# Attention with cached K and V: K loaded as four heads in 4 KB rows, V as one head per transfer

## The chip, the cores and the metric

The kernel runs on one core of a Trainium2 chip. A core has a matrix engine (TensorE, "PE" in the profile, with its weight loads as "PEld"), VectorE (DVE), ScalarE (ACT), GpSimd (POOL), a queue that mainly starts transfers (SyncE, SP) and 16 DMA engines that move data between the main memory and the core's SBUF. The metric is the time of one execution in device microseconds; a lower time is better.

## The reference

Two independent blocks, A and B, each compute an attention layer with a given cache:

```python
q = (x @ wq).reshape(B, Sq, H, Dh).transpose(0, 2, 1, 3)
scores = einsum("bhqd,bhkd->bhqk", q, k_cache) * (Dh ** -0.5)
p = softmax(scores, axis=-1)
o = einsum("bhqk,bhkd->bhqd", p, v_cache)
out = o.transpose(0, 2, 1, 3).reshape(B, Sq, H * Dh) @ wo
```

with B = 16 batches, Sq = 64 queries, D = 640, H = 32 heads, Sk = 512 keys and Dh = 128, all in bf16. The result is A's and B's output side by side, 16 x 64 x 1280. K and V of both blocks are 268 MB, each byte read once.

## The kernel before

**Steps.** A step works on one head of two batches, whose 2 x 64 queries fill 128 partitions. There are 512 steps: two blocks, two halves of 16 heads, eight pairs of batches, 16 heads. Two steps make a macro-step m (256 in all), and two macro-steps make a group of four heads, k (128 in all).

**One macro-step** goes through these operations, which the code names by short codes:

- LDK loads K (512 KB): two heads of two batches, on the partitions head by head with 64 partitions each, in rows of 8 keys, which are 2 KB. `kn_ring` has nine such buffers.
- KX (L586) transposes K on TensorE in 32 pieces of 64 rows of 128 elements, and KE (L593) copies the result from PSUM to `ktp_ring`, which has three slots (slot 0 for even m, slots 1 and 2 in turn for odd m).
- SM (L632) multiplies queries and transposed K, one matmul for each batch of a step, on two halves of the partitions; MX (L641) takes the negative row maximum on VectorE; EX (L647) takes the exponential on ScalarE and sums the rows; RC2 (L653) takes the reciprocals.
- NM (L661) on GpSimd multiplies the probabilities by the reciprocals and puts them into the order of the keys that V has on the partitions.
- TR2 (L670) transposes the probabilities on TensorE; TE and TA (L680, L684) copy them to SBUF.
- LDV loads V, one transfer of 512 KB for four heads of one batch, so two for each k: partition p holds keys 4p to 4p + 3 of each head, which is a row of 1 KB for each head. `v_ring` has five buffers for groups.
- PV2 (L694) multiplies V and the transposed probabilities; OE4 (L701) copies the result of four heads from PSUM.
- OP2 and OX (L709, L719) multiply by `wo`, and add up over 16 heads in PSUM; OVP, OXP, OVF, OXF and ST write out halves and sums.
- Q projections (QJ, QZ, QN, L603) and the transposes of x (XI, XT) stand in between.

**Order.** The order on each engine is written out by hand. `PHASES` holds, for a range of k, a template for each of TensorE, ScalarE, VectorE and GpSimd: operation, offset in macro-steps, sub-index and a time within a period. `build_plan` turns it into one list for each engine. All four SM groups of a k stand together at the start of its period.

**Transfers.** All loads are issued from the SP queue, in an order that `build_plan` works out from planned times (`STEP_US`, `DMA_US`, `START_US`): a load is due `LEAD` macro-steps before the operation that first needs it, not before its buffer is free. Each load is also tied to the TensorE operation that stands at its planned time ("paced"), so that SP waits for TensorE's progress. Waits are semaphores: each load adds 16 to the semaphore of its buffer when it has landed, and TensorE, which works in order, waits for it ahead of the operation that reads the buffer.

The two lines that matter for the shape of the V and K transfers are these:

```python
src = blocks[blk][2][2 * bp + m % 2, h0:h0 + G].rearrange("g (p t) d -> p g (t d)", p=128)
src = blocks[blk][1][2 * bp:2 * bp + 2, h0:h0 + 2].rearrange("j hs (p t) d -> (hs p) j (t d)", t=8)
```

Of the kernel before, what the change touches and what calls it, by code (L numbers as in the profile page):

```python
# [15 lines left out]
class Cfg:  # L16
    G = 4
# [5 lines left out]
    LEAD = 5.37  # L23
    WLEAD = 5.48
    STEP_US = ((8, 3.68), (32, 27.17), (160, 3.12), (216, 3.1), (256, 3.43))
    DMA_US = dict(LDK=1.40, LDV=1.44, LDWQ=1.8, LDWO=1.8, LDX=0.45, LDXR=0.5)
    START_US = 210.96
    BEFORE = 3.88
# [17 lines left out]
         (("OE4", -4, 0, 0.38), ("QEZ", 0, 0, 0.43), ("QEZ", 0, 1, 1.68), ("OVP", -1, 0, 2.62), ("QEZ", 0, 2, 2.72),  # L46
          ("EX", 1, 0, 2.78), ("QEZ", 0, 3, 3.12), ("QEZ", 0, 4, 3.5), ("EX", 1, 1, 3.54), ("QEZ", 0, 5, 3.88),
          ("EX", 0, 1, 4.51), ("OXP", -13, 0, 4.63), ("QEJ", 4, 0, 4.64), ("TA2", -2, 0, 4.76), ("EX", 0, 0, 5.06),
          ("QEZ", 0, 7, 5.11), ("QEN", -6, 0, 5.12), ("QEZ", 0, 6, 5.49), ("ST", -45, 0, 6.19)),
         (("KE", 4, 0, 0.07), ("XIE", 2, 1, 0.91), ("MX", 0, 0, 0.95), ("MX", 0, 1, 0.96), ("RC2", -1, 0, 0.99),  # L50
          ("MX", 1, 0, 1.46), ("OXF", 47, 0, 2.01), ("MX", 1, 1, 2.78), ("OVF", -23, 0, 3.45), ("TE2", -1, 0, 3.61),
          ("XIE", 2, 2, 3.73), ("XIE", 2, 3, 3.96), ("KE", 3, 0, 4.55), ("XIE", 6, 0, 4.58), ("XIE", 0, 4, 4.84),
          ("XIE", -4, 6, 4.98), ("XIE", -2, 5, 5.43), ("RC2", 0, 0, 5.63), ("XIE", 0, 7, 6.21)),
# [6 lines left out]
         (("OE4", -4, 0, 0.38), ("QEZ", 0, 0, 1.23), ("OXP", -13, 0, 1.5), ("EX", 0, 1, 1.52), ("OVP", -17, 0, 1.59),  # L60
          ("EX", 0, 0, 1.89), ("XTE", 28, 0, 2.28), ("QEZ", 0, 1, 2.45), ("QEN", -6, 0, 2.53), ("ST", -35, 0, 3.16),
# [22 lines left out]
          ("QEN", -6, 0, 3.07), ("TA2", -2, 0, 3.72), ("OXP", -3, 0, 4.37), ("OVP", -3, 0, 4.78), ("EX", 1, 1, 5.06),  # L84
          ("XTE", 0, 0, 5.27)),
         (("KE", 3, 0, 0.07), ("RC2", -1, 0, 0.53), ("MX", 0, 0, 1.15), ("MX", 0, 1, 1.7), ("MX", 1, 0, 1.78),
          ("KE", 2, 0, 2.61), ("MX", 1, 1, 3.18), ("RC2", 0, 0, 3.78), ("OXF", -3, 0, 4.23), ("TE2", -1, 0, 4.74),
          ("OVF", -3, 0, 5.58)),
# [9 lines left out]
          ("OXF", -3, 0, 6.18)),  # L98
# [12 lines left out]
    )  # L111
    TRB = (2, 3)
    OXB = 4
    OXH = False
    KTB = (6, 6)
    NWU = 32

# [22 lines left out]
def build_plan(dims, cfg):  # L140
# [73 lines left out]
    def bank(i):  # L214
        return ("PB", i)
# [173 lines left out]
    def sem_key(op):  # L389
        if op.kind in ("LDK", "LDV", "LDXR"):  # L390
            return ("d_" + op.kind[2:].lower(), op.writes[0][1])
# [542 lines left out]
```

## Time and profile before

| | |
|---|---|
| median of 3 runs | 850.43 us (849.04 to 854.05) |
| the profiled execution | 852.97 us |
| its span | 851.0 us |
| instructions | 38,366 |
| read from main memory | 292.03 MB |
| K: transfers, size, issue to landing (median, block A) | 128 per block, 512 KB, 6.5 us |
| V: transfers, size, issue to landing (median, block A) | 128 per block, 512 KB, 6.8 us |
| issue of one V transfer on SP (median) | 0.368 us |
| scores, L632 | 1,024 matmuls, mean 385 ns |
| normalizing, L661 | 512 on GpSimd, mean 843 ns |

The span is the time from the first to the last instruction of the one profiled execution; the execution's own time is 2 us longer. The table of the page counts busy time by engine; two engines can be busy at once, so shares don't add up to 100%. A packet is one contiguous row that one of the 16 DMA engines moves. The profile gives for each queue of the DMA engines the packets, the megabytes and the time its packets took, as a share of the span of all 16 engines; it can exceed 100% because packets of one engine may overlap a little.

### The profile page before, as it was taken

The page shows a single profiled execution, that of the slowest core. Times are in us where ns is not written, and L with a number is a line of the kernel's source. Part 1 is how long each engine was busy: PE and PEld are TensorE (multiplying, and loading weights), DVE is VectorE, ACT ScalarE, POOL GpSimd, SP SyncE. Part 2 cuts the span into 40 slices and gives each one's busy share as a digit, 9 for nine tenths or more (in the row PEclk, how much of TensorE's full clock was granted, in tenths as well). Part 3 has the DMA queues.
Part 4 walks back from the last instruction along what each step waited for, and adds up shares of the span by engine and source line. Part 5 has one row for each costly group of instructions (what it writes and reads, how often), then busy time and mean ns, then how long its engine had stood idle before and what let it go on. Part 6 is the DMA issues. An engine that isn't in the chain of part 4 may idle for free.

```text
span 851.0 us, 38366 instructions
## 1 busy us (share of the span) xinstructions
PE 811.3 (95%) x17025; PEld 566.4 (67%) x17156; DVE 727.9 (86%) x1192; ACT 644.7 (76%) x1466; POOL 417.1 (49%) x518
## 2 busy tenths in 40 slices
PE   8999999999999999999999998999999999999996
PEld 5566676666666666666666666666666666666664
DVE  4688888888888898888899887988888989989994
ACT  2678877777777787777877877787887877778886
POOL 0355455454544554454554545455455455455553
PEclk9999999999999999999999999999999999999999
DMA  9999999999999999999999999999999999999992
GB/s 306 360 354 349 369 354 352 348 338 362 354 352 353 369 369 363 359 360 367 364 362 367 364 360 349 321 362 362 360 360 363 366 369 365 366 339 352 370 321 89
DMA packets 228438, 297.14 MB, mean 349 GB/s; under 512 B 9136, under 2 KB 162736, under 8 KB 228272
## 3 DMA queue, kind: packets, MB, share of 16 engines
q1 hardware_dynamic: 225968, 292.06, 100.3%
q8 instruction: 134, 2.20, 1.1%
q10 hardware_dynamic: 2304, 2.62, 0.9%
q14 instruction: 32, 0.26, 0.1%
HBM read 292.03 MB, written 2.62 MB: 346 GB/s over the span
## 4 chain that ended last, share of the span: by engine, by line
PE 89%; issue 3%; ACT 3%; DMA 2%; DVE 2%; SPq 0%; ACTq 0%
PE ps L586 17%; PE ps L694 15%; PE ps L603 15%; PE ps L632 14%; PE ps L670 13%; PE ps L709 12%; PE ps L719 3%; ACT p_ring L647 2%; DMA v_ring<-in_A_v_cache_dram 1%; DVE negmax L641 1%; ACT pT_ring L684 1%; DMA wq_sb<-in_A_wq_dram 1%; DVE ktp_ring L593 1%; PE ps L804 0%; PE ps L813 0%
## 5 line engine op out<-in xcount | busy, mean ns | idle before, releaser
L661 POOL TENSOR_SCALAR pn_ring<-p_ring,recip 128x512 bf16<-128x512 bf16 x512 | 416.4, 843 | 425.1 <-DVE recip L653 379.0
L647 ACT ACTIVATE p_ring<-ps,negmax 128x512 bf16<-128x512 f32 x512 | 349.0, 688 | 74.0 <-DVE negmax L641 68.5
L593 DVE COPY ktp_ring<-ps 128x2048 bf16<-128x2048 bf16 x256 | 312.1, 1219 | 56.3 <-PE ps L586 56.2
L641 DVE TENSOR_REDUCE negmax<-ps 128x1 f32<-128x512 f32 x512 | 328.3, 683 | 16.2 <-PE ps L632 8.5
L586 PEld LDWEIGHTS ps<-ident,kn_ring 64*128 64x128 bf16 x8192 | 136.8, 95 | 107.9 <-issue 96.4
L586 PE MATMUL ps<-ident,kn_ring 64*128 64x64 bf16 x8192 | 169.2, 191 | 3.3 <-issue 1.4
L603 PE MATMUL ps<-xT_sb,wq_sb 128*128 128x512 bf16 (+2 forms) x543 | 133.4, 372 | 19.0 <-issue 18.1
L670 PEld LDWEIGHTS ps<-ident,pn_ring 128*128 128x128 bf16 x2048 | 125.4, 98 | 38.8 <-ACT p_ring L647 7.2
L694 PE MATMUL ps<-pT_ring,v_ring 128*128 128x64 bf16 x4096 | 143.5, 194 | 2.8 <-issue 1.9
L701 ACT ACTIVATE oT_ring<-ps 128x512 bf16<-128x512 f32 x128 | 76.4, 597 | 91.7 <-PE ps L694 91.7
L684 ACT ACTIVATE pT_ring<-ps 128x1024 bf16<-128x1024 bf16 (+1 forms) x144 | 140.9, 987 | 3.0 <-DVE pT_ring L680 2.2
L670 PE MATMUL ps<-ident,pn_ring 128*128 128x128 bf16 x2048 | 138.9, 219 | 3.4 <-issue 1.6
L709 PE MATMUL ps<-wo_sb,oT_ring 128*128 128x512 bf16 x498 | 135.3, 379 | 4.0 <-issue 1.9
L632 PE MATMUL ps<-ktp_ring,qc_ring 128*64 128x512 bf16 x1024 | 135.5, 385 | 0.7 <-issue 0.7
L694 PEld LDWEIGHTS ps<-pT_ring,v_ring 128*128 128x128 bf16 x4096 | 128.2, 98 | 9.6 <-issue 2.4
L647 ACT ACTIVATION_READ_ACCUMULATOR p_ring<-ps,negmax 128x1 f32 x512 | 104.8, 205 | 0.0
L680 DVE COPY pT_ring<-ps 128x1024 bf16<-128x1024 bf16 (+1 forms) x128 | 82.5, 644 | 14.6 <-PE ps L670 14.1
L619 ACT ACTIVATE qc_ring<-ps 128x512 bf16<-128x512 f32 (+1 forms) x129 | 76.8, 596 | 21.5 <-PE ps L603 21.4
L603 PEld LDWEIGHTS ps<-xT_sb,wq_sb 128*128 128x128 bf16 x660 | 53.8, 98 | 54.0 <-issue 1.1
L632 PEld LDWEIGHTS ps<-ktp_ring,qc_ring 128*64 128x64 bf16 x1024 | 47.2, 109 | 34.1 <-issue 1.3
L709 PEld LDWEIGHTS ps<-wo_sb,oT_ring 128*128 128x128 bf16 x512 | 42.7, 98 | 25.0 <-ACT pT_ring L684 2.1
L653 DVE RECIPROCAL recip<-rowsum 128x2 f32<-128x2 f32 x256 | 39.8, 155 | 4.4 <-ACT p_ring L647 4.4
(21 smaller groups left out, 127.2 us busy)
## 6 DMA issues: line engine op xcount, KB each, us to landing
kn_ring<-in_A_k_cache_dram SPq DMA_DIRECT2D x128, 512.0 KB, 6.5
v_ring<-in_A_v_cache_dram SPq DMA_DIRECT2D x128, 512.0 KB, 6.8
kn_ring<-in_B_k_cache_dram SPq DMA_DIRECT2D x128, 512.0 KB, 6.3
v_ring<-in_B_v_cache_dram SPq DMA_DIRECT2D x128, 512.0 KB, 6.5
wq_sb<-in_A_wq_dram SPq DMA_DIRECT2D x8, 640.0 KB, 7.1
wo_sb<-in_A_wo_dram SPq DMA_DIRECT2D x8, 640.0 KB, 7.2
wq_sb<-in_B_wq_dram SPq DMA_DIRECT2D x8, 640.0 KB, 6.8
wo_sb<-in_B_wo_dram SPq DMA_DIRECT2D x8, 640.0 KB, 6.6
```

The costliest lines, as they stand in the source:

```text
L586: last = e.transpose(kt_ps[hs][:, 64 * t:64 * t + 64], kn_ring[r, m % NKB, t // 8, t % 8 * DH:(t % 8 + 1) * DH], ident[r, r])
L593: ins = e.tensor_copy(ktp_ring[:, ktslot(op.idx)], ps[:, b:b + 2, :].rearrange("p b s -> p (b s)").bitcast(BF16))
L603: last = e.matmul(dst[:, col:col + n], wq_sb[:, qslot(hh // G), kt, (hh % G) * DH:(hh % G + 1) * DH], xT_sb[:, kt, lo * 128:hi * 128], sta ...
L632: ins = e.matmul(s_bank(g)[64 * j:64 * j + 64, :], q[:, 64 * j:64 * j + 64], kt[:, sub, j], start=True, stop=True, tile_position=(0, 64 * j))
L641: ins = e.reduce_max(negmax[:, r:r + 1], s_bank(g), axis=AX.X, negate=True)
L647: ins = e.activation(p_ring[:, g % NP, :], s_bank(g), ACTF.Exp, bias=negmax[:, r:r + 1], scale=1.0, accum_out=rowsum[:, r:r + 1])
L661: ins = e.tensor_scalar(dst, src, recip[:, r:r + 1], 1.0, ALU.mult, ALU.mult)
L670: ins = e.transpose(pt_flat(m)[:, (4 * sub + t) * 128:(4 * sub + t + 1) * 128], pn_ring[:, g % NPN, t * 128:(t + 1) * 128], ident[:, :])
L680: ins = e.tensor_copy(*pt_copy(op.idx, op.aux))
L684: ins = e.activation(*pt_copy(op.idx, op.aux), ACTF.Copy)
L694: ins = e.matmul(qo_ps[:, col:col + 64], v_ring[:, m // 2 % NVP, j, 2 * (m % 2) + sub, t * DH:(t + 1) * DH], pT_ring[:, m % NT, sub, t, 64 ...
L709: ins = e.matmul(out_ps, oT_ring[:, m // 2 % NO, 2 * (m % 2) + sub, :], wo_sb[:, wslot(ps_, hh // G), hh % G, 0:N0], start=(hh == 0), stop ...
```

## The change

Three things are changed together, with the order tables written anew.

- **K.** A K transfer now holds four heads of one batch, 32 partitions for each head, in rows of 16 keys, which are 4 KB. A macro-step's K buffer is thus no longer that of the macro-step's own two heads and two batches: the four heads of a k need both buffers of the pair, one for each batch. SM reads its head from two slots of `ktp_ring`, in 16 runs of 32 elements, and depends on both.
- **V.** A V transfer now holds one head of one batch (128 KB), so there are four times as many. Partition 32 th + p holds keys 16 p + 4 th to 16 p + 4 th + 3, which matches the order in which K's keys come out. PV2 waits for its own two heads of both batches only; a semaphore counts the four transfers of one PV2.
- **NM** writes the probabilities in four blocks of 32 for each run, instead of every second element.

The constants that plan the loads and the order tables are others; the sequence of operations within a period is nearly the same (for example OP2, OP2, OX where OP2, OX, OP2 stood).

```diff
-    LEAD = 5.37
-    WLEAD = 5.48
-    STEP_US = ((8, 3.68), (32, 27.17), (160, 3.12), (216, 3.1), (256, 3.43))
-    DMA_US = dict(LDK=1.40, LDV=1.44, LDWQ=1.8, LDWO=1.8, LDX=0.45, LDXR=0.5)
-    START_US = 210.96
-    BEFORE = 3.88
+    LEAD = 5.65
+    WLEAD = 5.95
+    STEP_US = ((8, 5.16), (32, 27.91), (160, 3.04), (216, 3.1), (256, 4.77))
+    DMA_US = dict(LDK=1.34, LDV=0.36, LDWQ=1.8, LDWO=1.8, LDX=0.45, LDXR=0.5)
+    START_US = 268.53
+    BEFORE = 4.65
...
         if kind == "SM":
-            return mk("pe", "SM", (m, sub), [qres(2 * m + sub), ("ktp", ktslot(m))], [bank(2 + (2 * m + sub) % cfg.NS)],
-                      ts)
+            return mk("pe", "SM", (m, sub), [qres(2 * m + sub), ("ktp", ktslot(2 * k)), ("ktp", ktslot(2 * k + 1))],
+                      [bank(2 + (2 * m + sub) % cfg.NS)], ts)
...
         if kind == "PV2":
-            return mk("pe", "PV2", m, [("pT", m % cfg.NT, 0), ("pT", m % cfg.NT, 1), ("v", k % cfg.NVP, 0), ("v", k % cfg.NVP, 1)], [bank(1)], ts)
+            return mk("pe", "PV2", m, [("pT", m % cfg.NT, i) for i in range(2)] + [("v", k % cfg.NVP, j, i) for j in range(2) for i in (g0 % G, g1 % G)], [bank(1)], ts)
...
-        add([("PV2", 2 * (k - cfg.NVP) + 1, 0)] if k >= cfg.NVP else [], ("PV2", 2 * k, 0), cfg.LEAD - j, 2, "LDV", m,
-            [("v", k % cfg.NVP, j)], m)
+        for i in range(G):
+            add([("PV2", 2 * (k - cfg.NVP) + i // 2, 0)] if k >= cfg.NVP else [], ("PV2", 2 * k + i // 2, 0), cfg.LEAD - j + i // 2, 2, "LDV", m,
+                [("v", k % cfg.NVP, j, i)], (m, i))
...
-        if op.kind in ("LDK", "LDV", "LDXR"):
+        if op.kind == "LDV":
+            return ("d_v", op.writes[0][1], op.aux[1] // 2)
+        if op.kind in ("LDK", "LDXR"):
...
-        kn_ring = sb("kn_ring", [128, NKB, 2, 8 * DH], BF16)
+        kn_ring = sb("kn_ring", [128, NKB, 16 * DH], BF16)
...
-            kt = ktp_ring[:, ktslot(m)].rearrange("p (hs j s) -> p hs j s", hs=2, j=2)
+            hd = 2 * (m % 2) + sub
...
+                kt = ktp_ring[:, ktslot(m // 2 * 2 + j)].rearrange("p (hs t h s) -> p hs t h s", hs=2, t=16, h=2)
                 ins = e.matmul(s_bank(g)[64 * j:64 * j + 64, :], q[:, 64 * j:64 * j + 64],
-                               kt[:, sub, j], start=True, stop=True, tile_position=(0, 64 * j))
+                               kt[:, hd // 2, :, hd % 2, :], start=True, stop=True, tile_position=(0, 64 * j))
...
-            src = p_ring[:, g % NP, :].rearrange("q (th tl pp) -> q th tl pp", th=2, tl=4)
-            dst = pn_ring[:, g % NPN, :].rearrange("q (tl pp th) -> q th tl pp", tl=4, th=2)
+            src = p_ring[:, g % NP, :].rearrange("q (th tl p) -> q th tl p", th=4, tl=4)
+            dst = pn_ring[:, g % NPN, :].rearrange("q (tl th p) -> q th tl p", tl=4, th=4)
...
-        def em_LDKV(e, op):
+        def em_LDK(e, op):
             m = op.aux
             blk, bp, grp, ps_, hh0 = step_info(2 * m)
             h0 = (ps_ % NHALF) * HH + hh0
-            if op.kind == "LDV":
-                h0 -= h0 % G
-                src = blocks[blk][2][2 * bp + m % 2, h0:h0 + G].rearrange("g (p t) d -> p g (t d)", p=128)
-                ins = e.dma_start(v_ring[:, m // 2 % NVP, m % 2], src)
-            else:
-                src = blocks[blk][1][2 * bp:2 * bp + 2, h0:h0 + 2].rearrange("j hs (p t) d -> (hs p) j (t d)", t=8)
-                ins = e.dma_start(kn_ring[:, m % NKB], src)
+            h0 -= h0 % G
+            src = blocks[blk][1][2 * bp + m % 2, h0:h0 + G].rearrange("h (p t) d -> (h p) (t d)", t=16)
+            ins = e.dma_start(kn_ring[:, m % NKB], src)
+            return ins, ins
+
+
+        def em_LDV(e, op):
+            m, i = op.aux
+            blk, bp, grp, ps_, hh0 = step_info(2 * m)
+            h = (ps_ % NHALF) * HH + hh0 - hh0 % G + i
+            src = blocks[blk][2][2 * bp + m % 2, h].rearrange("(p th t) d -> th p (t d)", th=4, t=4)
+            ins = e.dma_start(v_ring[:, m // 2 % NVP, m % 2, i], src)
             return ins, ins
```

More of the change, by code (lines that the diff above doesn't have):

```diff
@@ L39 @@
         (0,
[6 rows of a table removed]
[L46 to L53, printed above, removed]
[6 rows of a table removed]
-         (("OE4", -4, 0, 0.38), ("QEZ", 0, 0, 1.23), ("OXP", -13, 0, 1.5), ("EX", 0, 1, 1.52), ("OVP", -17, 0, 1.59),
-          ("EX", 0, 0, 1.89), ("XTE", 28, 0, 2.28), ("QEZ", 0, 1, 2.45), ("QEN", -6, 0, 2.53), ("ST", -35, 0, 3.16),
[22 rows of a table removed]
[L84 to L88, printed above, removed]
[9 rows of a table removed]
-          ("OXF", -3, 0, 6.18)),
[12 rows of a table removed]
[6 rows of a table added]
@@ new lines @@
+         (("OE4", -4, 0, 0.18), ("QEJ", 4, 0, 0.57), ("QEZ", 0, 0, 0.99), ("QEZ", 0, 1, 1.01), ("OVP", -9, 0, 2.27),
+          ("OXP", -7, 0, 2.33), ("EX", 1, 0, 2.75), ("QEZ", 0, 2, 3.35), ("QEZ", 0, 3, 3.38), ("ST", -53, 0, 3.41),
+          ("QEN", -6, 0, 3.77), ("EX", 1, 1, 3.84), ("QEZ", 0, 4, 4.01), ("EX", 0, 0, 4.55), ("QEZ", 0, 5, 4.62),
[3 rows of a table added]
+          ("XIE", 2, 2, 4.0), ("XIE", 2, 3, 4.35), ("XIE", 0, 4, 4.88), ("XIE", -4, 6, 5.23), ("XIE", 0, 7, 5.26),
[9 rows of a table added]
+          ("QEZ", 0, 2, 3.95), ("QEN", -6, 0, 4.46), ("EX", 1, 0, 4.8), ("OXP", -17, 0, 4.94), ("QEZ", 0, 3, 5.01),
+          ("EX", 1, 1, 5.79)),
+         (("MX", 0, 0, 0.18), ("OVF", -55, 0, 0.84), ("KE", 3, 0, 1.07), ("MX", 0, 1, 1.09), ("RC2", -1, 0, 1.12),
+          ("MX", 1, 0, 2.53), ("KE", 2, 0, 4.46), ("MX", 1, 1, 4.62), ("TE2", -1, 0, 4.76), ("RC2", 0, 0, 4.98),
+          ("OXF", 13, 0, 5.18)),
[7 rows of a table added]
+          ("OXP", -3, 0, 6.17), ("OVP", -3, 0, 6.24)),
[10 rows of a table added]
+          ("TA2", -2, 0, 3.63), ("QEN", -6, 0, 3.77), ("OVP", -3, 0, 4.49), ("EX", 1, 1, 5.23), ("OXP", -3, 0, 5.9),
+          ("XTE", 0, 0, 6.28)),
+         (("KE", 3, 0, 0.68), ("MX", 0, 0, 0.9), ("RC2", -1, 0, 0.91), ("MX", 0, 1, 1.47), ("MX", 1, 0, 2.66),
+          ("KE", 2, 0, 2.72), ("MX", 1, 1, 2.95), ("RC2", 0, 0, 4.13), ("TE2", -1, 0, 4.82), ("OVF", -3, 0, 5.04),
+          ("OXF", -3, 0, 5.65)),
[9 rows of a table added]
+          ("OXF", -3, 0, 5.93)),
[9 rows of a table added]
+          ("OXF", -77, 0, 5.93)),
+         (("NM", -1, 1, 3.23), ("NM", -1, 0, 4.58), ("NM", 0, 0, 5.12), ("NM", 0, 1, 6.06))),
@@ L585, in em_KX @@
                     r = slice(64 * hs, 64 * hs + 64)
-                    last = e.transpose(kt_ps[hs][:, 64 * t:64 * t + 64], kn_ring[r, m % NKB, t // 8, t % 8 * DH:(t % 8 + 1) * DH],
+                    last = e.transpose(kt_ps[hs][:, 64 * t:64 * t + 64], kn_ring[r, m % NKB, t * DH:(t + 1) * DH],
                                        ident[r, r])
@@ L839, in mha_kernel @@
                         OVP=em_OVP, OXP=em_OXP, OVF=em_OVF, OXF=em_OXF, ST=em_ST, INIT1=em_INIT1, INIT2=em_INIT2,
-                        LDWQ=em_LDWQ, LDWO=em_LDWO, LDX=em_LDX, LDXR=em_LDXR, XT=em_XT, XTE=em_XTE, XI=em_XI, XIE=em_XIE, WU=em_WU, LDK=em_LDKV, LDV=em_LDKV)
+                        LDWQ=em_LDWQ, LDWO=em_LDWO, LDX=em_LDX, LDXR=em_LDXR, XT=em_XT, XTE=em_XTE, XI=em_XI, XIE=em_XIE, WU=em_WU, LDK=em_LDK, LDV=em_LDV)
         def full(s, v):
```

98 rows, old and new, of the table PHASES are left out of this document.

## The prediction

> **What bounds the kernel now.** I read the page's first three parts, then the waits and the chain, then the DMA traffic of a stretch in the middle, and last the trace's record of single packets.
>
> ```profile
> PE 811.3 (95%) x17025; PEld 566.4 (67%) x17156; DVE 727.9 (86%) x1192; ACT 644.7 (76%) x1466; POOL 417.1 (49%) x518
> DMA  9999999999999999999999999999999999999992
> DMA packets 228438, 297.14 MB, mean 349 GB/s; under 512 B 9136, under 2 KB 162736, under 8 KB 228272
> q1 hardware_dynamic: 225968, 292.06, 100.3%
> PE 89%; issue 3%; ACT 3%; DMA 2%; DVE 2%; SPq 0%; ACTq 0%
> ```
>
> The reader is to see two resources that are full at once. TensorE is busy for 811.3 of 851.0 us and makes 89% of the chain. The 16 DMA engines carry packets for 100.3% of the span. TensorE hardly waits for them: the longest waits of this kind in the list of waits are 1.2 us (wq_sb, at the start) and 0.9 us (v_ring), once each, and of the longer waits of the SP queue nearly all are for TensorE, since the loads are paced by it. So the loads just keep up. A middle stretch shows how closely:
>
> ```profile
> 400.00:500.00 100.00, 97.16 (x2059) 67.61 (x2072) 89.23 (x146) 76.48 (x175) 50.45 (x62) 1.00 1.06 364
> ```
>
> Here PE (first figure after the length) is 97% busy at full clock, and DMA moves 364 GB/s with packet times that add up to 1.06 of its engines' time.
>
> The trace records each packet. Medians: 46 ns for 1 KB (44 at least), 55 for 1,280 B, 84 for 2 KB, 307 for 8 KB (the shortest), 1,085 for the 16 KB of instruction code, 9 for the 4 bytes that end an engine's share of a load. They are the same with three packets in flight as with twenty, so I read them as what one engine spends on one packet. Check on 400 to 500 us, which holds 19,026 packets of 1 to 1.25 KB, 7,778 of 2 KB, 1,137 ends and 16 of code: 19,026 x 46.7 + 7,778 x 84 + 1,137 x 9 + 16 x 1,085 = 1,570 us, over 16 engines 98 us of the 100. The medians explain a full queue.
>
> The 9,136 packets under 512 B are those ends. The kernel issues 571 transfers (256 K, 256 V, 32 weight tiles, 11 of x, 16 stores), and 571 x 16 = 9,136: every transfer of before runs on all 16 engines. In each of them both sides have 128 as their outermost dimension.
>
> **The change, part by part.**
>
> *V loads (LDV).* A transfer of 512 KB becomes four of 128 KB: 256 become 1,024, still of 1 KB rows, 131,072 packets. What is new is the shape of the source: the rows are taken as th (4) x p (32) x 1 KB, and in the built program the DRAM side reads 4 x 32 x 512 elements against 128 x 512 in SBUF. All other transfers keep 128 outermost on both sides. A transfer must be cut so that an engine's part of the source matches its part of the destination; along the outermost dimensions, 4 and 128, there are only four such parts. Every row of before fits a cut along the outermost dimension; none shows one that goes into an inner dimension, as sixteen parts of 4 x 32 would need. The built program also drops, on these 1,024 transfers alone, a mark that every other one carries. I therefore take the cut into four as the likely one: V then runs on 4 of the 16 engines.
>
> [...]
>
> The four engines' work, each of them:
> - V: 131,072 / 4 x 46 ns = 1,507 us (before: 131,072 / 16 x 46 = 377).
> - K, cut over 16 as before, now 32,768 packets of 4 KB. No row has 4 KB; between 84 (2 KB) and 307 (8 KB) a straight line gives 158, and bounds are 2 x 84 = 168 and 307 / 2 = 153. I take 159: 2,048 x 159 = 326 us (before 4,096 x 84 = 344), with 313 to 344.
> - wq 640 x 46 = 29; wo, x and stores 768 x 55 = 42; ends (1,024 + 315) x 9 = 12; code 134 / 16 x 1,085 = 9.
>
> Sum 1,925 us, against some 807 for each engine before.
>
> [...]
>
> *Path and covers.* Around that sum: about 2 us before the first packet and 2 us in which the early loads, which wait for TensorE, leave engines idle (DMA share 0.90 in the first 20 us); at the end about 2 us until the last load's semaphore, and what follows the last L694 group, at 844.7 of 851.0, so 6.3 us. Span 1,925 + 12 = 1,937. The profiled execution took 852.97 for its span of 851.0, and the median of the runs is 850.43: +2.0 - 2.5. I say 1,940.
>
> The four engines don't run dry: V's loads are paced about five macro-steps ahead of use, and while TensorE stands at a PV2 the loads of some two more batches of four heads (8 x 32 x 46 + 2 x 8 x 159 = 14.3 us of queue each) are already issued. One ring on SP feeds both kinds, so K's share on these engines lies behind V's and K comes late too. V late means PV2 (L694 before) waits on TensorE's in-order queue; behind it stand the next scores, K transposes and Q projections, for which VectorE, ScalarE and GpSimd wait. All of them idle together.
>
> *Scores (SM)* read K^T in 16 runs of 32 elements instead of one run of 512, and need both slots of a pair of K blocks. All four SM groups of a pair already run back to back after both K copies, so the second adds no wait. No row has such a read: bounds are no change and a doubling of 135.5 us. I take none, as nearest to what both forms are, one element a column. *NM* writes runs of 32 instead of every second element: 843 ns now, bounds half and double (+-432 us on GpSimd). I take none. *K transposes, V's semaphores, the new order tables and start times*: the same instructions in nearly the same order. All of this lies under the DMA sum: TensorE at 811 + 135 and GpSimd at 863 are 1,000 us from it; even all of TensorE's work at half clock (the granted mean was 0.91 in the first 20 us) would be 1,622. *SP issues* 768 more transfers; at 0.368 us (median of L789) 1,323 of them are 487 us, covered twice over even if V's take double. Without the DMA cover they matter (third rival).
>
> **Rivals.**
> 1. *V still runs on 16 engines* (the other side: not slower). For it: all 571 transfers of before do. Against: none has unlike sides. It decides as soon as a V load ends in 16 pieces. Then each engine carries 795 us instead of 807 (K 18 less, 768 x 9 ns = 7 more), and TensorE keeps 811 busy; it gets back part of the start's wait for V, 11.65 us of the chain. 839 to 851, I say 845.
> 2. *Four engines, but a lone engine packs 1 KB rows at the 8 KB rate* (38 ns): 1,258 + 313 + 92 + 12 = 1,675. For it: packet times add up to 1.06 of the engines' time in full stretches, so packets overlap a little. Against: 46 is the median at any number in flight.
> 3. *16 engines, and SP's issue becomes the bound.* A group of four heads takes 851 / 128 = 6.65 us, less 0.86 for K and the rest, over 8 V issues: above 0.72 us each, SP sets the pace. Rows: 0.368, back to back 0.47; an unmarked form is not shown. At 0.83 us each, 128 x 7.5 = 960; at twice 0.47, 1,073.
>
> **From this to the numbers.** Forecast 0.83, rival 1 0.08, rival 2 0.04, rival 3 0.05. The forecast's own spread: 44 ns and K at 153 give 1,855; the means (49.4 for 1 KB, 91.2 for 2 KB) instead of the medians give 1,619 + 354 + 100 + 12 = 2,085; if the 6% overlap is all pipelining, 1,925 / 1.06 + 12 = 1,828. Range 1,800 to 2,110, which leaves out the three rivals and little else: about 0.8. A difference under 0.5% can't be told from none here. Slower: forecast, rivals 2 and 3, 0.92; rival 1 splits into 0.05 faster and 0.03 within 0.5%.
>
> **What would show it.** Four engines: V's ends fall to 4 a load, 4,096 + 315 x 16 = 9,136 in all (by chance the old count; with 16 it would be 21,424); the DMA row near 4 tenths (12,610 us of packets / 16 / 1,937) at some 153 GB/s; V's issue to landing from 6.7 to some 30 us or more; TensorE near 42% busy with waits for v_ring at PV2, and v_ring leading the chain. K's rows: packets under 2 KB unchanged near 162,700, and 65,536 of 2 KB become 32,768. SM's mean (385 ns) and NM's (843) test the two zeros. The forecast is wrong if the ends are 21,424 or the DMA row stays at 9. If the ends are right and the time is not, the price of a 1 KB packet on an engine is.

## The result, and the profile after

| | before | after |
|---|---|---|
| median of the runs | 849.73 us (848.61 to 854.05) | 1,934.16 us (1,931.45 to 1,940.68) |
| span of the profiled execution | 851.0 us | 1,933.4 us |

The ratio is 2.275 (95% interval 2.265 to 2.285): the changed kernel takes 1,084 us more. The forecast was 1,940 us. From here on an execution that took over 1.5% longer than the fastest of its kernel is left out of a time, which concerns one of four of the kernel with 16 x 8 x 512 (1,153 us with it, as later expectations have it) and two of four of the kernel with V in quarters.

The first three parts of the changed kernel's page, in the lines that were shown of before:

```profile
PE 1100.4 (57%) x17156; PEld 724.5 (37%) x17156; DVE 744.3 (38%) x1192; ACT 667.7 (35%) x1466; POOL 349.7 (18%) x518
...
PEclk8777777777777777777777777777777777777776
DMA  7544454444554444444445444444445444444442
...
DMA packets 195676, 297.19 MB, mean 154 GB/s; under 512 B 9136, under 2 KB 162736, under 8 KB 195504
...
q1 hardware_dynamic: 193200, 292.06, 46.2%
```

Neither resource is full any more by these lines: the DMA row stands at 4 and 5 tenths where it stood at 9, and TensorE is busy for 57% (at a mean granted clock of 0.744 instead of 0.998, so its busy time grew from 811 to 1,100 us without any more work). A mean over 16 engines hides what happens here: by the prediction's estimate, four engines that are full and twelve that carry only K's share and the rest come to 41%, and the queue stands at 46.2%. The line that tells is the number of packets under 512 B, the ends of transfers: 9,136 = 1,024 x 4 + 315 x 16. With 16 engines for each V transfer it would be 21,424.

The wait itself, in TensorE's order of work in the changed kernel (start, length, engine, line, operation, how often; in brackets the idle time before it and what ended it):

```profile
902.02 0.64 PE L589 MATMUL ps<-ident,kn_ring 64*128 64x64 bf16 x31
909.71 0.23 PE L589 MATMUL ps<-ident,kn_ring 64*128 64x64 bf16 x1 [7.05 <-DMA v_ring<-in_A_v_cache_dram]
909.88 1.89 PE L698 MATMUL ps<-pT_ring,v_ring 128*128 128x64 bf16 x32
911.70 1.92 PE L636 MATMUL ps<-ktp_ring,qc_ring 128*64 128x512 bf16 x8
```

TensorE stands still for 7.05 us here, between the 31st and the 32nd transpose of K. The wait belongs to PV2 (L698): where an operation has two waits, the kernel hangs one on the last instruction of the operation ahead of it. So the list of waits (total, times, longest) books most of it on L589:

```profile
PE ps L589 <- DMA v_ring<-in_B_v_cache_dram: 314.1, 48, 11.3
PE ps L589 <- DMA v_ring<-in_A_v_cache_dram: 311.9, 48, 10.0
...
PE ps L698 <- DMA v_ring<-in_B_v_cache_dram: 100.4, 16, 7.9
...
PE ps L698 <- DMA v_ring<-in_A_v_cache_dram: 82.8, 13, 8.9
```

That is 809 us in 125 waits, one for nearly each of the 128 groups of four heads. The chain of the changed kernel, by engine:

```profile
SPq 75%; DMA 13%; PE 8%; issue 3%; ACT 0%; DVE 0%
```

By line, 52% of it is L801, where SP issues V, 22% is L792, where it issues K, and 13% is V's transfers. So the chain names not the transfers but their issue. This allows another reading than the forecast's, namely that issuing V in its new form is slow by itself. The first experiments tell these two apart.

### The profile page after: what moved, and what is told of

Same layout as the page of the kernel before. It is cut to its first block, busy times and chain, and to the rows that moved or that the text cites. A ratio compares the mean times of both kernels' runs of the same rounds, so it can differ in the third digit from the quotient of the medians.

```text
span 1933.4 us, 39279 instructions
## 1 busy us (share of the span) xinstructions
PE 1100.4 (57%) x17156; PEld 724.5 (37%) x17156; DVE 744.3 (38%) x1192; ACT 667.7 (35%) x1466; POOL 349.7 (18%) x518
## 2 busy tenths in 40 slices
DMA packets 195676, 297.19 MB, mean 154 GB/s; under 512 B 9136, under 2 KB 162736, under 8 KB 195504
## 3 DMA queue, kind: packets, MB, share of 16 engines
q1 hardware_dynamic: 193200, 292.06, 46.2%
## 4 chain that ended last, share of the span: by engine, by line
SPq 75%; DMA 13%; PE 8%; issue 3%; ACT 0%; DVE 0%
SPq L801 52%; SPq L792 22%; DMA v_ring<-in_A_v_cache_dram 7%; DMA v_ring<-in_B_v_cache_dram 7%; PE ps L698 2%; PE ps L636 2%; PE ps L589 1%; PE ps L606 1%; PE ps L674 1%; SPq L777 1%; PE ps L713 1%; SPq L806 1%; DMA wq_sb<-in_A_wq_dram 0%; SPq L769 0%; PE ps L723 0%
## 5 line engine op out<-in xcount | busy, mean ns | idle before, releaser
L665 POOL TENSOR_SCALAR pn_ring<-p_ring,recip 128x512 bf16<-128x512 bf16 x512 | 349.0, 695 | 1561.8 <-DVE recip L657 1363.0
L589 PE MATMUL ps<-ident,kn_ring 64*128 64x64 bf16 x8192 | 213.2, 204 | 626.0 <-DMA v_ring<-in_B_v_cache_dram 314.1
L645 DVE TENSOR_REDUCE negmax<-ps 128x1 f32<-128x512 f32 x512 | 335.5, 682 | 342.4 <-PE ps L636 342.4
L589 PEld LDWEIGHTS ps<-ident,kn_ring 64*128 64x128 bf16 x8192 | 168.3, 104 | 768.5 <-DMA v_ring<-in_B_v_cache_dram 319.8
L651 ACT ACTIVATE p_ring<-ps,negmax 128x512 bf16<-128x512 f32 x512 | 350.1, 687 | 102.3 <-DVE negmax L645 98.3
L698 PE MATMUL ps<-pT_ring,v_ring 128*128 128x64 bf16 x4096 | 241.5, 241 | 183.3 <-DMA v_ring<-in_B_v_cache_dram 100.4
L698 PEld LDWEIGHTS ps<-pT_ring,v_ring 128*128 128x128 bf16 x4096 | 221.6, 131 | 198.9 <-DMA v_ring<-in_B_v_cache_dram 103.1
L636 PE MATMUL ps<-ktp_ring,qc_ring 128*64 128x512 bf16 x1024 | 235.9, 613 | 0.0
L606 PE MATMUL ps<-xT_sb,wq_sb 128*128 128x512 bf16 (+2 forms) x660 | 177.3, 407 | 2.9 <-DMA wq_sb<-in_A_wq_dram 2.7
L713 PE MATMUL ps<-wo_sb,oT_ring 128*128 128x512 bf16 x512 | 141.7, 390 | 13.5 <-DMA v_ring<-in_A_v_cache_dram 12.8
L674 PEld LDWEIGHTS ps<-ident,pn_ring 128*128 128x128 bf16 x2048 | 128.1, 99 | 36.8 <-issue 2.1
L674 PE MATMUL ps<-ident,pn_ring 128*128 128x128 bf16 x2048 | 139.6, 220 | 1.0 <-ACT pT_ring L688 1.0
L651 ACT ACTIVATION_READ_ACCUMULATOR p_ring<-ps,negmax 128x1 f32 x512 | 102.4, 200 | 0.0
L636 PEld LDWEIGHTS ps<-ktp_ring,qc_ring 128*64 128x64 bf16 x1024 | 69.0, 158 | 74.6 <-issue 63.0
```

What stands on the lines that cost most here:

```text
L589: last = e.transpose(kt_ps[hs][:, 64 * t:64 * t + 64], kn_ring[r, m % NKB, t * DH:(t + 1) * DH], ident[r, r])
L606: last = e.matmul(dst[:, col:col + n], wq_sb[:, qslot(hh // G), kt, (hh % G) * DH:(hh % G + 1) * DH], xT_sb[:, kt, lo * 128:hi * 128], sta ...
L636: ins = e.matmul(s_bank(g)[64 * j:64 * j + 64, :], q[:, 64 * j:64 * j + 64], kt[:, hd // 2, :, hd % 2, :], start=True, stop=True, tile_pos ...
L645: ins = e.reduce_max(negmax[:, r:r + 1], s_bank(g), axis=AX.X, negate=True)
L651: ins = e.activation(p_ring[:, g % NP, :], s_bank(g), ACTF.Exp, bias=negmax[:, r:r + 1], scale=1.0, accum_out=rowsum[:, r:r + 1])
L665: ins = e.tensor_scalar(dst, src, recip[:, r:r + 1], 1.0, ALU.mult, ALU.mult)
```

## The experiments

### How the time follows the outermost count of V's source

Three kernels change one line of the changed kernel, the order in which a V transfer reads its 128 rows of 1 KB. Number, size and destination of the transfers stay, and so do K, NM and the order tables.

```diff
-            src = blocks[blk][2][2 * bp + m % 2, h].rearrange("(p th t) d -> th p (t d)", th=4, t=4)
+            src = blocks[blk][2][2 * bp + m % 2, h].rearrange("(p th t) d -> th p (t d)", th=16, t=4)
```

for 16 x 8 x 512, and th=8 and th=2 for the others. "Unlike sides" in the expectations means that the source and the destination of a transfer are laid out with different counts (16 x 8 rows against 128, say). The "mark" is the flag of the built program that the prediction speaks of; in the kernels here every transfer with like sides carries it and every one with unlike sides lacks it.

> The changed kernel, but the source of a V transfer is read as 16 x 8 x 512 elements instead of 4 x 32 x 512: still 1,024 transfers of 128 KB in 1 KB rows, still with unlike sides and without the mark; only its outermost count differs. V's keys then lie on other partitions than P's, so the output mixes keys. Theory 1 (the transfer is cut along the outermost count, V ran on four engines): 16 engines again, 795 us of packets each, TensorE bounds, 840 to 865 us, 21,424 packets under 512 B. Theory 2 (SP's issue of this unlike form bounds: in the changed kernel the median V issue took 1.34 us and SP leads the chain with 75%): the same 1,024 issues of the same form, so about 1,900 us again.

> As the kernel with 16 x 8 x 512, with 8 x 16 x 512 (the output mixes keys). Theory 1: V on eight engines, each 131,072 / 8 x 46 ns = 754 us for V, 2,048 x 159 ns = 326 for K and 92 for the rest, plus 12 around it: 1,184 us, 13,232 packets under 512 B. Theory 2: about 1,900 us again.

> The same with 2 x 64 x 512 (the output mixes keys). Theory 1: V on two engines, 131,072 / 2 x 46 ns = 3,015 us for V, 326 for K, 92 for the rest and 12 around it: 3,445 us, 7,088 packets under 512 B. Theory 2: about 1,900 us again.

| source | packets under 512 B | engines by that | 1 KB packet, median (mean) | V issue on SP, median | time |
|---|---|---|---|---|---|
| 2 x 64 | 7,088 | 2 | 46 (47.1) ns | 2.63 us | 3,262.9 us |
| 4 x 32 (the change) | 9,136 | 4 | 46 (48.9) ns | 1.34 us | 1,934.2 us |
| 8 x 16 | 13,232 | 8 | 46 (55.8) ns | 0.74 to 0.81 us | 1,354.7 us |
| 16 x 8 | 21,424 | 16 | 69 (70.6) ns | 0.60 us | 1,149.6 us |

The kernels with 2 x 64 and 8 x 16 ran once each, so their times have no spread; the differences are far larger than any spread seen here.

Packets and queue at the two ends of this table, from the page of 16 x 8 and then of 2 x 64:

```profile
DMA packets 207964, 297.24 MB, mean 259 GB/s; under 512 B 21424, under 2 KB 175024, under 8 KB 207792
...
q1 hardware_dynamic: 205488, 292.11, 103.5%
```

```profile
DMA packets 193628, 297.18 MB, mean 91 GB/s; under 512 B 7088, under 2 KB 160688, under 8 KB 193456
...
q1 hardware_dynamic: 191152, 292.06, 27.2%
```

The ends come out to the packet as theory 1 says in all four rows: the outermost count of the source, 2, 4, 8 or 16, is the number of ends of a V transfer, and so of the engines. Theory 2 falls: with the same 1,024 issues of the same form, the time went from 3,263 to 1,150 us. Nor is one issue of this form slow by itself: the shortest took 0.53, 0.55, 0.60 and 0.54 us with 2, 4, 8 and 16 engines. At the median an issue on SP takes about as long as the engines need for a transfer (32 packets x 46 ns = 1.47 us on four engines, 1.34 measured; 64 x 46 ns = 2.94 us on two, 2.63 measured), and I read that as SP held up by a full queue; the profile shows the length of an issue, not the queue. By this reading the 52% of the chain in the changed kernel are the four engines' time, seen from the other end of the queue.

The sizes were less exact than the ends. 2 x 64 came out 5% under what was expected, 8 x 16 14% over it; the point on the sum, further below, works out why. And 16 x 8, at 1,149.6 us (ratio 1.356, 1.345 to 1.366), was a miss: 840 to 865 was expected. There all 16 engines are full (103.5%), because a packet takes 69 ns instead of 46. This called for the next runs.

### V on 16 engines, in its natural order

In the first kernel V is read in the order of memory and NM keeps its blocks of 32. In the second NM also writes every fourth element, so that P's keys stand in V's order (the first pair of lines is in both kernels, the second pair in the second alone).

```diff
-            src = blocks[blk][2][2 * bp + m % 2, h].rearrange("(p th t) d -> th p (t d)", th=4, t=4)
+            src = blocks[blk][2][2 * bp + m % 2, h].rearrange("(p t) d -> p (t d)", t=4)
...
-            dst = pn_ring[:, g % NPN, :].rearrange("q (tl th p) -> q th tl p", tl=4, th=4)
+            dst = pn_ring[:, g % NPN, :].rearrange("q (tl p th) -> q th tl p", tl=4, th=4)
```

> The changed kernel with one thing undone: V's source is read in its natural order, 128 rows on both sides (and marked), still 1,024 transfers of one head; NM keeps its blocks of 32, so V's keys lie on other partitions than P's and the output mixes keys. If the cut over the engines and the form of that cut are all that costs: packets at 46 and 159 ns, 795 us for each engine, TensorE bounds, 840 to 865 us. If four times as many transfers cost by themselves (SP or the ends): about 900 or more, with TensorE waiting for v_ring.

> The changed kernel with V read in its natural order, 128 rows of four keys, still one head a transfer (1,024), and NM writing every fourth element so that P's keys stand in V's order. Computes the whole reference. Theory 1: 16 engines, as the kernel with 16 x 8 x 512, 839 to 860 us; at 0.47 us an issue SP needs 1,024 x 0.47 + 299 x 0.37 = 592 us and is hidden. Theory 2: the form is marked again, issues at 0.37 to 0.47 us, also about 850; it does not tell the two apart. If NM with a step of four elements (843 ns with a step of two, 695 ns in runs of 32) takes more than about 1,600 ns, GpSimd bounds above 851 us.

The first took 848.63 us against 851.86 us of the kernel before on the same chip, ratio 0.9956 (0.9927 to 0.9985). Its page:

```profile
PE 808.1 (95%) x17010; PEld 569.3 (67%) x17156; DVE 725.4 (86%) x1192; ACT 652.8 (77%) x1466; POOL 349.9 (41%) x518
...
DMA  8999999999999999999999999999999999999992
...
DMA packets 207964, 297.24 MB, mean 351 GB/s; under 512 B 21424, under 2 KB 175024, under 8 KB 207792
...
q1 hardware_dynamic: 205488, 292.11, 98.5%
...
PE 83%; ACT 8%; DVE 3%; issue 3%; DMA 2%; POOL 0%; SPq 0%; ACTq 0%
```

All that the change brings is in this kernel except V's shape: the 4 KB rows of K, the strided scores, NM in blocks, 1,024 V transfers, the new order. TensorE is at 95% again, packets are at 46 and 159 ns (medians), and SP is gone from the chain. With V's shape undone the whole 1,084 us are gone, so the other parts of the change make none of them. V's new shape in the kernel before, with K as it was, was not run.

The second took 974.32 us, ratio 1.146 (1.141 to 1.151), where 839 to 860 was expected. Its packets are at 46 ns; its NM is slow. First the group of NM, then two of the waits of this kernel:

```profile
L665 POOL TENSOR_SCALAR pn_ring<-p_ring,recip 128x512 bf16<-128x512 bf16 x512 | 680.4, 1414 | 281.1 <-DVE recip L657 233.7
```

```profile
ACT p_ring L651 <- POOL pn_ring L665: 141.1, 111, 1.3
PEld ps L674 <- POOL pn_ring L665: 109.1, 111, 1.5
```

At 1,414 ns NM stays under the 1,600 ns from which GpSimd would be full (an estimate from 851 us for 512 of them), and it bounds all the same: the exponentials (L651) and the transposes of P (L674) now wait for it 111 times each, and GpSimd has 34% of the chain. The limit in that expectation came from GpSimd's busy time alone. The waits point to the length of one NM in an order that was written out for a shorter one; a run with another order, which would show it, was not made.

### Why 16 engines were not always enough

Three more edits of the changed kernel follow. The first two read 32 x 4 x 512 and were meant to differ in the order of addresses. The third cuts V by quarters of the partitions; there PV2 waits for all four quarters of a batch, where the changed kernel waits for its own two heads (these lines are not shown).

```diff
+            src = blocks[blk][2][2 * bp + m % 2, h].rearrange("(th p t) d -> p th (t d)", th=4, t=4)
...
+            src = blocks[blk][2][2 * bp + m % 2, h].rearrange("(p th t) d -> th p (t d)", th=32, t=4)
...
+            src = blocks[blk][2][2 * bp + m % 2, h0:h0 + G].rearrange("g (p th t) d -> th p g (t d)", th=4, t=4)[i]
+            ins = e.dma_start(v_ring[32 * i:32 * i + 32, m // 2 % NVP, m % 2], src)
```

> As the kernel with 16 x 8 x 512, which took 1,153 us with 1 KB packets at a median of 69 ns, but with the source read as 32 x 4 x 512 in steps of 1 KB and 128 KB of which the outer 32 are neighbours (the output mixes keys). Unlike sides and no mark again; 32 can be cut into 16. [...] Theory b (the pattern of addresses in main memory slowed the packets): another pattern, so another price, 46 ns and about 850 us if it was only that.

> As the kernel with 16 x 8 x 512 (1,153 us, 1 KB packets at 69 ns), with 32 x 4 x 512: neighbouring kilobytes of the source again go to the outermost dimension, and one step of the inner one is 32 KB (there 16 KB). Unlike sides, no mark, 16 engines; the output mixes keys. The kernel with another 32 x 4 x 512 had 46 ns and 961 us. If the outer count (16 or 32, and with it the partitions each engine writes) made the 69 ns: 46 ns and about 960 us. If the order of addresses in main memory did: about 69 ns and 1,150 us.

> The changed kernel with V cut the other way: a transfer holds a quarter of the partitions (32) for four heads of one batch, 32 x 4 x 512 on both sides, marked, 1,024 transfers of 128 KB as before. Computes the whole reference with NM in blocks of 32. Theory 1 alone (16 engines, 46 ns): TensorE bounds, 840 to 860 us. [...]

The first two are one and the same kernel: both lines give an outer step of 1 KB and an inner step of 32 KB (the first expectation's 128 KB is a slip), and the programs built from them are equal. So 960.6 and 951.3 us are two executions of it, with a median of 46 ns for a 1 KB packet in both. The quarters took 1,245.4 us, ratio 1.462 (1.445 to 1.480), with 78 ns a packet and a full queue. The queue of 32 x 4 (second execution), then that of the quarters:

```profile
q1 hardware_dynamic: 205488, 292.11, 92.8%
```

```profile
q1 hardware_dynamic: 205488, 292.11, 103.8%
```

Not every unlike form slows the packets: 16 x 8 has 69 ns, and 32 x 4 is unlike too and has 46. What does slow them stays open. From 16 x 8 to 32 x 4 the outer count changes, but the inner step goes from 16 KB to 32 KB at the same time, so the order of addresses (theory b) has not been tried by itself, and neither is excluded. In the quarters a transfer writes 32 partitions only, and its rows are 4 KB and its heads 128 KB apart, so there too both change. Which partitions an engine writes isn't in the profile, so no run here shows why a packet of the quarters takes 78 ns.

32 x 4 loses 100 us with packets at 46 ns, and SP is the first place to look. Issues of V, first with th=32, then in the natural order of above (minimum, median and maximum in ns), and last the chain with th=32:

```profile
L801 SPq DMA_DIRECT2D v_ring<-in_A_v_cache_dram x512: 534/603/1685, 14.2 to 483.3; - x171
```

```profile
L801 SPq DMA_DIRECT2D v_ring<-in_A_v_cache_dram x512: 327/432/1622, 14.2 to 431.7; - x171
```

```profile
PE 40%; SPq 36%; DMA 18%; issue 3%; ACT 1%; DVE 1%; ACTq 0%
```

An issue of the unlike form takes 0.171 us longer, and 1,024 of them 175 us. From 400 to 500 us SP goes from issue to issue without a stop of more than 0.34 us; in the natural order its stops add up to 16 us there. SP has 36% of the chain (0% in the natural order). This is the prediction's third rival, alive in a kernel that has its 16 engines. But in the same stretch the DMA share is 0.97 and TensorE is 90% busy, so that SP makes the whole 100 us is likely, not shown.

### K's part and V's part by themselves

K's part is the changed kernel with V's transfers as they were before:

```diff
+            src = blocks[blk][2][2 * bp + m % 2, h0:h0 + G].rearrange("g (p t) d -> p g (t d)", p=128)
+            ins = e.dma_start(v_ring[:, m // 2 % NVP, m % 2], src)
```

> K's part of the change alone: K in 4 KB rows with SM's runs of 32, NM in blocks of 32, the new order tables, but V as before in 256 transfers of four heads with 128 rows on both sides (V's keys lie on other partitions than P's, so the output mixes keys). By the prediction's terms K's longer rows take 18 us off each DMA engine's 807 and TensorE keeps its work: 839 to 851 us. If the longer rows or the strided read of K cost something hidden by the V change: above 855.

V's part is the kernel before with one head for each V transfer:

```diff
-                src = blocks[blk][2][2 * bp + m % 2, h0:h0 + G].rearrange("g (p t) d -> p g (t d)", p=128)
-                ins = e.dma_start(v_ring[:, m // 2 % NVP, m % 2], src)
+                src = blocks[blk][2][2 * bp + m % 2, h0 + i].rearrange("(p t) d -> p (t d)", t=4)
+                ins = e.dma_start(v_ring[:, m // 2 % NVP, m % 2, i], src)
```

> The kernel before with V's part alone and without its new order: 1,024 transfers of one head, each 128 rows of 1 KB on both sides, marked. Computes the whole reference. The prediction costs 768 more ends at 9 ns, 7 us for each engine of 807, and 768 more issues at 0.37 to 0.47 us, hidden: 850 to 860 us. If many small marked transfers cost more than that: 870 or more, with SP ahead of TensorE in the chain.

K's part took 857.43 us, ratio 1.0066 (1.0042 to 1.0091), where 839 to 851 was expected. That is in the range that the expectation kept for a hidden cost of the longer rows or the strided read, yet neither shows in its row: the scores take 385 ns, as before, and NM 695. V's split took 854.62 us, ratio 1.0041 (1.0022 to 1.0061), within its 850 to 860. Each alone is a little slower than before, and both together (848.63 us, above) a little faster. Both of these kernels run with start times of loads that were worked out for other transfers, which may be the reason; it was not tried apart, so this half per cent stays open. What they do show is that neither makes more than about 6 of the 1,084 us.

### The order of the keys made by the scores

K comes in 4 KB rows and V in the transfers of before, NM does not reorder, and the scores read K^T so that the keys come out in V's order.

```diff
-                kt = ktp_ring[:, ktslot(m // 2 * 2 + j)].rearrange("p (hs t h s) -> p hs t h s", hs=2, t=16, h=2)
+                kt = ktp_ring[:, ktslot(m // 2 * 2 + j)].rearrange("p (hs th tl h s) -> p hs h tl s th", hs=2, th=4, tl=4, h=2)
```

> K in 4 KB rows as in the changed kernel, V in its natural order in 256 transfers of four heads as in the kernel before, NM without any reordering (one run of 512), and the order of the keys made by the scores instead: SM reads K^T element by element with a step of 512 bytes in groups of four. Computes the whole reference. If TensorE reads such a pattern at its full rate, SM stays at 385 ns and the time is 835 to 855 us, with NM under 695 ns. If it doesn't, SM doubles or worse: 851 + 135 = 986 us or more.

It took 1,243.9 us, ratio 1.461 (1.453 to 1.469). The scores of this kernel, by group:

```profile
L633 PE MATMUL ps<-ktp_ring,qc_ring 128*64 128x512 bf16 x1024 | 539.6, 1185 | 0.0
```

A matmul of 385 ns becomes one of 1,185 when neighbouring columns, in groups of four, lie 512 bytes apart. The busy time of the scores grows from 135.5 to 539.6 us, by 404, and the kernel's time by 392. No kernel tried that computes the whole reference beats the one before.

## Why the prediction was right, point by point

- **V on four engines.** Right, and now shown: 9,136 ends, and 2, 4, 8 or 16 engines by one number in one line. Ahead of the runs the four was the author's estimate: every transfer of before had 128 outermost on both sides and 16 ends, so none showed it. Why a transfer is cut at that count no run shows.
- **The sum, 1,925 us for each of the four engines.** Measured span 1,933.4, less the 12 us that were put around it: 1,921. The prices held as medians: 46 ns for 1 KB, 159 for K's 4 KB. That the sum comes so close is luck, for two things that it leaves out cancel. One is the packets slower than the median: with the means of this trace (48.9 ns for 1 KB, 200.6 for 4 KB, 106 us for the rest) the sum is 2,121 us. The other is that packets on one engine overlap, as packet times of 1.06 times the engines' time in before (400 to 500 us) show: these 2,121 us fit into 1,921, which is a factor of 1.10. The same working gives 3,613 us against the 3,249 that the span leaves with two engines, and 1,483 against 1,341 with eight, 1.11 both times, so by this estimate the overlap is about a tenth in all three. The prices of the sum, which miss both, come out 6% too high with two engines (3,433 us) and 13% too low with eight (1,172), where the slow packets weigh more. The trace doesn't give a packet's engine, so K's mean is that of all 16. Why packets are slow isn't shown. The prediction's spread held both effects, one at a time; its case with 44 ns adds up to 1,858 us and not to 1,855, which changes nothing.
- **The DMA row.** 154 GB/s for 153; queue share 46% where medians gave 41% in all, since it holds the slow packets too (K's above all, a mean of 201 ns for a median of 159).
- **TensorE near 42%.** It was 57%, because the granted clock fell to a mean of 0.744 (0.998 before). The working had kept half clock as a case that stays covered, and it did.
- **"V's issue to landing to some 30 us", K late, "v_ring leading the chain".** This is the step that was wrong, without harm to the time: the queue was thought to stand on the engines, and by the trace the time passes on SP. An issue of V held SP for 1.34 us at the median (0.55 at the shortest), so the chain is booked on SP (75%), and what had been issued landed soon. K's transfers landed 9.3 us after their issue (6.5 before). For V the page gives no landing time, but the semaphore's increments in the trace do for the last of the four transfers that share a wait: 9.5 us at the median, 7.8 to 11.2, and not some 30.
- **Scores at no cost.** Right: 387 ns against 385 in the kernel with V in natural order, at a granted clock of 0.99. **NM at no cost:** it fell to 695 from 843 ns, off the path. **768 more issues hidden:** right for marked ones at 0.43 us.
- **The rivals.** The first, 845 us, did not happen, but its working was sound: with 16 engines the same kernel takes 848.63. The second is there in part, as the overlap of a tenth. The third shows in another kernel, at a median of 0.60 us an issue, which is under the 0.72 us from which the prediction let SP set the pace. The mean is 0.67, and K's issues take 0.59 us there (0.43 in the natural order), where the working had them and the rest at 0.86 us for a whole group of four heads.

## What to carry to other kernels

Before a transfer's shape is changed, compare the outermost counts of its two sides, and count the packets under 512 B in the profile: here, with 2, 4, 8 and 16 as the outermost count of its source, a V transfer had as many of them. A mean DMA share of 46% is no proof of spare bandwidth, and a chain that ends on the issuing queue may be the far end of a few full engines (SP with 75% here). A reordering that comes free in one place can be dear in another: by GpSimd in steps of four elements, by the scores and by the partitions of a transfer it took 974, 1,244 and 1,245 us.

## What the runs showed of the hardware

- With 16 engines a 1 KB packet took 46, 69 or 78 ns by how a transfer was shaped (128 or 32 outermost; 16 x 8; 32 partitions at a time); K's 4 KB packets in the same kernels took 159, 233 and 258 (medians). The cause isn't settled.
- With 16 engines an issue on SP of 128 KB took 0.43 us at the median where both sides begin with 128, and 0.60 where they are unlike and the program lacks the mark; the two go together here.
- With V on 2, 4 and 8 engines, the mean packet times of an engine's share add up to 1.11, 1.10 and 1.11 times the time it had. Read as an overlap of packets on one engine, this is about a tenth, an estimate from the means of all 16 engines: the trace doesn't give a packet's engine.
- A V transfer on four engines raised its semaphore five times: the trace has 10,160 increments = 1,024 x 5 + 315 x 16. That is one increment more for each such transfer than it has ends, and the first increment of four transfers comes 1.25 us after the first issue begins (median), against 3.5 us with 16 engines in natural order. What the additional one adds isn't shown.
- GpSimd's multiplication of 128 x 512 took 695 ns writing runs of 32, 697 writing one run of 512, 843 writing every second element and 1,414 writing every fourth.
